# Mirrored inverse rows in both halves of a gated convolution and MLP kernel, with scratch moved and the order lists made anew

## Chip, cores and metric

The kernel runs on one core of one Trainium2 chip. The metric is device time in microseconds (us) for one execution. Times of a kernel are given as the median of its runs; the profile shows one execution.

## The reference, cut

```python
x = A_q                                   # [1, 2048, 640], bf16
g = sigmoid((x * gate_w).sum(-1, keepdims=True))
# A: short causal filter, long causal convolution per channel
k_shift = sum_t k_pad[:, t:t+S, :] * shift_k[:, ks-1-t]      # 4 taps
kv = k_shift * v
y  = irfft(rfft(pad(kv)) * rfft(pad(ssm_k)))[:S] + kv * ssm_D
a  = q * y
# B: layernorm, gelu MLP with shifted column groups, then a second MLP
h  = gelu(layernorm(x) @ w1)              # 640 -> 640
x1 = x + shift_groups(h) @ w2             # groups moved by +1, -1, +2, -2 rows
b  = x1 + gelu(layernorm(x1) @ w3) @ w4   # 640 -> 1536 -> 640
out = g * a + (1 - g) * b
```

## The kernel before

The whole work lies in one SBUF tensor ("arena") with fixed regions. Rows are numbered by r = row mod 8, so each of the 16 row tiles (c = 0, 1 and r = 0 to 7) holds 128 rows.

Branch B is a chain of matrix products: mm1 (layernorm(x) @ w1), mm2 (@ w2), a second layernorm, mm3 (@ w3, line 1064) and mm4 (@ w4, line 1035). The four parts of mm3 and mm4 (sc = 0 to 3) are cut into jobs on TensorE, evicted by ScalarE (line 582).

Branch A does the long convolution by a hand-made transform. The channels are cut into two halves of 320 columns, and each half goes through two parts (kap 0 and 1). Stage numbers in the tags are 2 * half + kap, so stages 0 and 1 are half 0 and stages 2 and 3 are half 1. The steps for a half are:

- forward: TensorE multiplies the taps (h) and kv (k) with a table (line 1093), ScalarE evicts into slots
- window and butterfly (tags win, bhd, bha, bht, bhs for h; bkd, bka, bkt, bks for k): sums and differences of rows on VectorE (line 551)
- product (tags pwT and pwS): the two complex products, with a scratch area "temp" and a result area. An addition inside may be an accumulating DMA on POOL's queue (line 1123; pwTa, pwTb, pwSa, pwSb). The last two instructions of a product (tags ending in z and y) read the scratch
- fold (foldd, folda, foldt, folds): more sums and differences. Where it is done whole, some instructions go through a helper that joins two areas (line 1209)
- inverse (line 1279): for each r0 = 0 to 7, TensorE multiplies rows of the two parts with a table. ScalarE evicts with the gate (gy) into one of four buffers, VectorE multiplies by q (fin) and adds to branch B (finx, or an accumulating DMA fina; finl for the last rows, after mm4 of part 3). An output DMA follows.

A slot has 16 rows of 320 columns. Slots s0 to s4, t0 and t1 lie flat. Slots k0 and k1 are the two column halves of kv's region, so each row of 320 values (640 bytes) is followed by a gap of the same length. The letters a and b name the first and last 8 rows of a slot. q's columns of half 0 are loaded into k0, and of half 1 into k1, by two loads each on SP's queue (line 594); the load for the b rows stands first.

The inverse of a half in EVEN is mirrored: two VectorE passes of 2560 elements (tags mir and mira) form the difference and the sum of the two parts' even rows, and the four even r0 then take two matmul terms of two matmuls each instead of four terms:

```python
mirrored = half in EVEN
if mirrored:
    tt(hs(temp), Y0[0], Y1[0], ALU.subtract, 2560, tag="mir")
    add(Y0[0], Y1[0], 2560, ("mir", half) in BY_DMA, "mira")
```

The fold of part 1 writes its rows in swapped pairs where its half is in EVEN. Scratch for half 1's work depends on half 0:

```python
spare = ("k0a", "k1a", "s1a") if 0 in EVEN else ("s4a", "s4a", "s4a")
units(1, (..., ("pw", 0, spare[0], "s0a", "s4b", "t1a"),
          ..., ("pw", 1, spare[1], "s4b", "t0a", "s3a"), ("fold", 1, "s3b", spare[2])))
inverse(0, Y[0][0], Y[0][1], "s4a")
inverse(1, Y[1][0], Y[1][1], "s3b")
```

The order of all instructions is written out by hand: every operation is a node with its number in order of creation, RANK gives each node its place (highest first), each engine runs its own nodes in that order, and PAIR gives each matmul job one of four pairs of PSUM banks. Semaphore waits follow from which bytes each node reads and writes. Fill matmuls (line 647) stand ahead of the first real work on TensorE.

Of the kernel before, what the change touches and what calls it, by code (L numbers as in the profile page):

```python
# [292 lines left out]
def _bf16_bits(a):  # L293
# [4 lines left out]

FILL = 0
FILLN = 1  # L300
# [14 lines left out]
EVEN = ()  # L315
# [4 lines left out]
EVEN = ()  # L320
# [3 lines left out]
EVEN = (1,)  # L324
# [2 lines left out]
BY_DMA = BY_DMA | {("pwb", 1, 0), ("pwb", 1, 1)}  # L327
R4M = {("h",1),("k",1)}
FILL = 96
PW_SPLIT = ((1, 1),)  # L330
FOLD_SPLIT = ((1, 1),)
LN2_ACT = (2, 3)
RANK = [
# [45 lines left out]
]  # L379
PAIR = [  # L380
# [7 lines left out]
]  # L388

def _freq(kap):  # L390
# [38 lines left out]
def bass_gated_mix__ssm_conv_h3__mixer_s_mlp__prompt_kernel(  # L429
# [98 lines left out]
    def bank(pair, b, n, o=0):  # L528
        c = (2 * pair + b) * 512
        return PS[:, c + o:c + o + n]  # L530
# [113 lines left out]

    for i in range(FILL):
        P.stage = i * 8 // FILL
        P.pe([(lambda e, ps: e.matmul(bank(ps, 0, 128), ones, ones, start=True, stop=True)) for _ in range(FILLN)], r=[ones],
# [674 lines left out]
    def bydma(what, half, kap):  # L1322
        return (what, half, kap) in BY_DMA
# [4 lines left out]
    def units(half, plan):  # L1328
        for step in plan:
# [7 lines left out]
            elif what == "pw":  # L1337
                parts["y"] = [product(parts["bh"][i], parts["bk"][i], step[2 + 2 * i], step[3 + 2 * i],
                                      bydma("pwa", half, kap), bydma("pwb", half, kap), (half, kap) not in PW_SPLIT, "pw" + "TS"[i]) for i in range(2)]
            else:  # L1340
# [55 lines left out]
```

## Time and profile before

| | us |
|---|---|
| median of 3 runs | 227.44 (226.01 to 230.68) |
| the profiled execution | 224.98 |
| its span in the profile | 222.8 |
| TensorE (PE) busy | 214.7 |
| VectorE (DVE) busy | 205.7 |
| ScalarE (ACT) busy | 169.2 |
| GpSimd (POOL) busy | 54.7 |

The span runs from the first to the last instruction of the profiled execution; its time lies 2.2 us above its span. Busy times of one engine's instructions are added without their overlaps. In the groups by line, a helper's line stands for all operations that go through it: 551 for VectorE's two-input operations, 582 for ScalarE's evictions, 1123 for accumulating DMAs, 594 for loads. Lines 1035 (mm4), 1064 (mm3), 1093 (forward) and 1279 (inverse) are the matmuls by job.

### The profile page before, as it was taken

To read this page: it belongs to the slowest core of one execution; us is meant where nothing else is said; L and a number is where in the kernel's file an instruction comes from. 1 tells how busy PE (TensorE), PEld (TensorE's weight loads), DVE (VectorE), ACT (ScalarE), POOL (GpSimd) and SP (SyncE) were. 2 spreads that over 40 slices of the span, in tenths; PEclk is the share of its full clock that TensorE was granted. 3 is DMA by queue.
4 is the path that set the end of the run, shared out by engine and by line. 5 is a ranking of instruction groups with operands and counts; after the bars stand their busy time and mean duration, and the time that the engine had idled before them with its cause. 6 is when DMAs were issued, how large, how long until landed. Compare 5 with 4: busy or idle time off the path is not lost.

```text
span 222.8 us, 3922 instructions
## 1 busy us (share of the span) xinstructions
PE 214.7 (96%) x1533; PEld 135.4 (61%) x1533; DVE 205.7 (92%) x285; ACT 169.2 (76%) x287; POOL 54.7 (25%) x64
## 2 busy tenths in 40 slices
PE   7999999999998899999999999999999999999993
PEld 7749675457666564446765555577554676565671
DVE  2999999999998999999999999999985999998973
ACT  4598997799999999989988998880268342586660
POOL 1143094143015011704200110232310340317200
PEclk9999999999999999999999999999999999999998
DMA  6999985849983778674160154489686489956968
GB/s 205 384 406 389 399 327 105 207 113 259 140 232 108 219 193 299 149 214 90 29 122 0 32 89 87 66 130 188 120 183 174 89 146 175 257 102 107 128 213 261
DMA packets 41578, 39.75 MB, mean 178 GB/s; under 512 B 20452, under 2 KB 34791, under 8 KB 41432
## 3 DMA queue, kind: packets, MB, share of 16 engines
q1 hardware_dynamic: 33864, 24.75, 39.2%
q0 software_dynamic: 7408, 14.42, 31.2%
q10 hardware_dynamic: 288, 0.33, 0.4%
q8 instruction: 12, 0.20, 0.4%
q14 instruction: 6, 0.05, 0.1%
HBM read 21.60 MB, written 3.93 MB: 115 GB/s over the span
## 4 chain that ended last, share of the span: by engine, by line
DVE 49%; PE 32%; DMA 9%; issue 5%; ACT 3%; DVEq 0%; ACTq 0%
DVE arena L551 40%; PE PS L1064 13%; PE PS L1035 9%; PE PS L1093 7%; DMA arena<-arena 7%; DVE arena L778 5%; ACT arena L582 3%; DVE arena L556 2%; PE PS L973 2%; DMA arena<-in_A_q_dram 2%; PE PS L1279 1%; DVE arena L780 1%; DVE arena L1209 1%; ACT PS L955 0%; DVE arena L1048 0%
## 5 line engine op out<-in xcount | busy, mean ns | idle before, releaser
L551 DVE TENSOR_TENSOR arena<-arena 128x1280 bf16<-128x1280 bf16 (+6 forms) x178 | 170.4, 1010 | 7.3 <-DMA arena<-arena 4.9
L582 ACT ACTIVATE arena<-PS 128x640 bf16<-128x640 f32 (+7 forms) x140 | 101.8, 796 | 14.3 <-PE PS L1064 7.3
L1064 PE MATMUL PS<-arena 128*128 128x512 bf16 x240 | 54.3, 379 | 0.2
L1035 PE MATMUL PS<-arena 128*128 128x320 bf16 x384 | 54.3, 299 | 0.1
L582 ACT ACTIVATE arena<-PS,arena 128x320 bf16<-128x320 f32 (+1 forms) x48 | 26.1, 589 | 28.7 <-PE PS L1035 11.8
L1035 PEld LDWEIGHTS PS<-arena 128*128 128x128 bf16 x384 | 37.5, 98 | 15.1 <-issue 0.4
L1123 POOL DMA_DIRECT2D arena<-arena x24 | 24.0, 1172 | 81.3 <-DVE arena L551 75.2
L1064 PEld LDWEIGHTS PS<-arena 128*128 128x128 bf16 x240 | 22.9, 98 | 27.4 <-ACT arena L582 1.2
L1093 PE MATMUL PS<-arena 128*128 128x320 bf16 x208 | 32.3, 299 | 0.4 <-DVE arena L551 0.3
L1093 PEld LDWEIGHTS PS<-arena 128*128 128x128 bf16 x208 | 19.7, 98 | 10.8 <-ACT arena L582 1.1
L568 ACT ACTIVATE arena<-arena 128x640 bf16<-128x640 bf16 (+2 forms) x30 | 22.7, 758 | 2.6 <-DMA arena<-in_A_q_dram 2.2
L973 PE MATMUL PS<-arena 128*128 128x320 bf16 x160 | 22.7, 299 | 1.3 <-ACT PS L955 1.3
L863 PE MATMUL PS<-arena 128*128 128x512 bf16 (+1 forms) x125 | 23.6, 337 | 0.0
L955 ACT ACTIVATE PS<-arena 128x640 f32<-128x640 bf16 x32 | 22.7, 713 | 0.4
L758 POOL TENSOR_TENSOR arena<-arena 128x4 f32<-128x4 f32 (+1 forms) x9 | 13.8, 1531 | 37.0 <-DVE arena L556 34.0
L973 PEld LDWEIGHTS PS<-arena 128*128 128x128 bf16 x160 | 15.2, 98 | 8.6 <-ACT PS L955 2.3
L1279 PE MATMUL PS<-arena 128*128 128x320 bf16 x112 | 17.2, 299 | 0.6 <-DVE arena L551 0.3
L863 PEld LDWEIGHTS PS<-arena 128*128 128x128 bf16 x125 | 11.7, 98 | 9.3 <-ACT arena L582 0.7
L778 DVE BATCH_NORM_STATS2 arena<-arena 128x6 f32<-128x320 bf16 x28 | 12.1, 473 | 3.5 <-DMA arena<-in_A_q_dram 3.5
L1279 PEld LDWEIGHTS PS<-arena 128*128 128x128 bf16 x112 | 10.6, 98 | 6.6 <-ACT arena L582 1.1
L556 DVE TENSOR_SCALAR arena<-arena 128x640 bf16<-128x640 bf16 (+3 forms) x36 | 12.5, 366 | 1.2 <-POOL arena L758 1.0
L903 POOL DMA_DIRECT2D arena<-arena x18 | 9.8, 550 | 10.7 <-ACT arena L582 10.7
(40 smaller groups left out, 77.0 us busy)
## 6 DMA issues: line engine op xcount, KB each, us to landing
arena<-arena POOLq DMA_DIRECT2D x18, 320.0 KB, 4.5
arena<-in_B_w_dram POOLq DMA_DIRECT2D x4, 960.0 KB, 6.4
arena<-in_A_k_dram SPq DMA_DIRECT2D x4, 640.0 KB, 13.1
arena<-in_A_v_dram SPq DMA_DIRECT2D x4, 640.0 KB, 14.1
arena<-arena POOLq DMA_DIRECT2D x4, 640.0 KB, 6.5
arena<-in_A_q_dram SPq DMA_DIRECT2D x4, 640.0 KB, 7.3
out_dram<-arena SPq DMA_DIRECT2D x15, 160.0 KB, 2.0
arena<-in_A_q_dram SPq DMA_DIRECT2D x6, 320.0 KB, 5.1
```

What stands on the lines that cost most here:

```text
L551: return dve(lambda e: e.tensor_tensor(o, a, b, op), [a, b], [o], c_tt(n), tag=tag, **kw)
L568: node = P.op("act", lambda e, ps: e.activation(o, i, func, **kw), r=r, w=[o], cost=c_act(n, naps, acc is not None, psum=False), tag=tag, ...
L582: node = P.op("act", lambda e, ps: e.activation(ov, inner(ps), func, **kw), r=r, w=[o], cost=c_act(n, len(r), acc is not None), job=job, t ...
L778: dve(lambda e, o=o, x=x: e.bn_stats(o, x), [x], [o], 0.393, tag="bn", group=("bn", id(mv), rho, c))
L863: fns.append(lambda e, ps, b=b, c=c, lhsT=lhsT: e.matmul(bank(ps, b, 256 * n), lhsT, XT[:, c, r0:r0 + n, :], start=(c == 0), stop=(c == 4)))
L955: P.seed(job, lambda e, ps: e.activation(two(ps, 320), x, ACTF.Copy), [X[:, c, rho, :]], c_act(640, psum=False), tag)
L973: fns.append(lambda e, ps, hh=hh, ft=ft, lhsT=lhsT: e.matmul(bank(ps, hh, 320), lhsT, w2v[:, ft, 320 * hh:320 * hh + 320], start=False, st ...
L1035: fns.append(lambda e, ps, hh=hh, ft=ft, lhsT=lhsT: e.matmul(bank(ps, hh, 320), lhsT, w4h[ft // 6][:, ft % 6, 320 * hh:320 * hh + 320], st ...
L1064: fns.append(lambda e, ps, b=b, ft=ft, c=c, sc=sc: e.matmul(bank(ps, b, 512), w3h[ft // 6][:, c, 128 * (ft % 6):128 * (ft % 6) + 128], XT[ ...
L1093: fns.append(lambda e, ps, w=w, b=b, rhs=rhs, st=(first and n == 0), en=(n == len(ss) - 1): e.matmul(bank(ps, b, 320), w, rhs, start=st, s ...
L1123: return P.dma("pool", lambda e, ps: e.dma_start(o, i, accum_op=ALU.add, max_dma_last_dim=2560), r=[o, i], w=[o], nbytes=nb, cost=1.2, kin ...
L1279: fns.append(lambda e, ps, w=w, z=z, c=c, st=(n == 0), en=(n == len(terms) - 1): e.matmul(bank(ps, c, 320), w, z[:, c, :], start=st, stop=en))
```

## The change

Half 0 is mirrored like half 1. With it the scratch of half 1's first complex product goes from s4a to k0a (stage 2) and k1a (stage 3), a result area of half 1's second fold goes from s4a to s1a, and s4a holds half 0's difference rows. Half 0's second fold writes its rows in swapped pairs. Two nodes are added (955 become 957), the 244 jobs stay, and both lists are new. Cut diff:

```diff
 FILL = 96
+EVEN = (0, 1)
 PW_SPLIT = ((1, 1),)
 FOLD_SPLIT = ((1, 1),)
 LN2_ACT = (2, 3)
 RANK = [
-    951, 950, 940, 954, 946, 953, 929, 934, 923, 892, 910, 866, 848, 948, 916, 939, 790, 872, 781, 898, 825,
...
+    954, 953, 942, 956, 949, 941, 931, 921, 926, 892, 886, 861, 814, 950, 900, 948, 776, 875, 807, 906, 802,
...
 ]
 PAIR = [
-    0, 1, 2, 2, 2, 1, 0, 3, 3, 2, 2, 2, 1, 0, 1, 1, 2, 2, 3, 1, 2, 3, 0, 0, 3, 2, 3, 3, 1, 1, 2, 0, 1, 0, 3, 3,
...
+    0, 0, 3, 2, 0, 0, 3, 1, 3, 1, 3, 1, 3, 0, 0, 3, 3, 3, 2, 0, 3, 2, 3, 0, 2, 3, 3, 2, 3, 2, 0, 3, 0, 2, 0, 1,
...
 ]
```

VectorE's order from the second half's first butterfly on, before and after, by tag and stage (x counts what stands in a row):

```
before: bhd:2 win:2 folds:1 bht:2x2 win:2 bkd:2 bkt:2 bhd:3 bkt:2 pwT:2 bhs:2 pwT:2x2 bhs:2 pwT:2 bks:2x2 bht:3
  pwS:2x4 bht:3 win:3 pwTy:2 win:3 bht:3 pwTz:2 pwSy:2 bht:3 bhs:3 pwSz:2 bkd:3 foldd:2 bkt:3x4 pwT:3 bhs:3 foldd:2
  bhs:3 pwT:3x4 bks:3x3 fin:0 bhs:3 pwT:3 bks:3 fin:0 pwS:3x5 pwTy:3 pwS:3 pwTz:3 foldt:2 foldd:3 folds:2 pwSz:3
  pwSy:3 foldd:3 foldt:3x2 fin:0x2 folds:3x2 mir:1 mira:1 fin:1x4 finx:1 finl:3x2 ...
after: bhd:2 win:2 bht:2 folds:1 win:2 bht:2 bkd:2 bkt:2 mir:0 mira:0 bhd:3 bkt:2 bhs:2 pwT:2 win:3 bhs:2 pwT:2x3
  bks:2x2 bht:3 pwS:2 bht:3 pwS:2x3 bhs:3 bht:3 bhs:3 pwTy:2 pwTz:2 bht:3 win:3 pwSy:2 pwSz:2 bkd:3 bkt:3x2 foldd:2
  bkt:3x2 foldd:2 pwT:3x4 fin:0 bks:3x2 bhs:3 bks:3 bhs:3 bks:3 pwT:3 pwS:3x5 fin:0 pwT:3 pwTy:3 pwTz:3 foldt:2 pwS:3
  foldd:3 pwSz:3 pwSy:3 foldd:3 folds:2 foldt:3x2 fin:0x2 finl:3 folds:3 fin:1x2 folds:3 mir:1 finl:3 mira:1 ...
```

100 rows, old and new, of tables (PAIR, RANK) are left out of this document.

## Prediction

> **What bounds the kernel now.** I read the page first, then the busy time cut into four stretches, then the waits of VectorE and the chain of waits, and at last the stretch after 139 us instruction by instruction.
>
> ```profile
> span 222.8 us, 3922 instructions
> PE 214.7 (96%) x1533; PEld 135.4 (61%) x1533; DVE 205.7 (92%) x285; ACT 169.2 (76%) x287; POOL 54.7 (25%) x64
> 0.00:71.00 71.00, 68.62 (x615) 47.09 (x615) 66.00 (x101) 61.62 (x109) 21.29 (x33) 1.00 0.84 257
> 71.00:139.70 68.70, 67.31 (x410) 39.03 (x411) 66.70 (x86) 64.18 (x110) 12.96 (x12) 1.00 0.50 124
> 139.70:209.70 70.00, 69.68 (x446) 43.16 (x445) 65.12 (x80) 38.04 (x59) 20.47 (x20) 1.00 0.79 146
> 209.70:222.80 13.10, 9.05 (x66) 6.08 (x63) 7.93 (x20) 5.33 (x11) 0.00 (x0) 0.95 0.72 213
> ```
>
> The columns of the stretches are length, then busy us of PE, weight loads, DVE, ACT and POOL, then clock, DMA share and GB/s. There are two full lanes. TensorE lacks 0.32 us between 139.7 and 209.7 and 1.39 us in the stretch before; VectorE lacks 4.88 us and 2.00 us. Shortening one lane alone buys little, so the change has to be priced on both. Where VectorE idles:
>
> ```profile
> DVE arena L551 <- DMA arena<-arena: 4.9, 4, 3.2
> DVE arena L778 <- DMA arena<-in_A_q_dram: 3.5, 1, 3.5
> DVE arena L556 <- POOL arena L758: 1.0, 1, 1.0
> DVE arena L551 <- PE PS L1093: 0.2, 1, 0.2
> ```
>
> The 4.9 us are waits for accumulating DMAs, and the chain of waits of the last 60 us shows three of them (start, length):
>
> ```profile
> 160.69 1.50 DVE arena L551
> 162.19 0.28 issue
> 162.48 6.87 DMA arena<-arena
> ...
> 191.91 5.67 DMA arena<-arena
> ...
> 200.39 3.60 DMA arena<-arena
> ...
> 205.80 1.50 DVE arena L551
> 207.32 0.71 DVE arena L551
> ...
> 210.71 0.72 PE PS L1279 x4
> 211.43 1.63 PE PS L1035 x12
> ...
> 215.78 3.27 PE PS L1035 x24
> 219.07 0.55 DVE arena L1048
> ```
>
> The instructions at 205.80 and 207.32 are the two mirror passes of half 1 (mir, mira). After them TensorE works through mirrored inverse jobs and half jobs of mm4 until 219.05; a last VectorE instruction and an output DMA end the span at 222.8.
>
> **The change, TensorE lane.** Half 0's four even rows get two terms of two matmuls each where they had four terms: 16 matmuls of 320 columns go. Their price is read from spacing, not from the mean duration, as they overlap:
>
> ```profile
> 143.80 2.34 PE L1279 MATMUL PS<-arena 128*128 128x320 bf16 x16
> 145.97 13.20 PE L1035 MATMUL PS<-arena 128*128 128x320 bf16 x96
> 159.01 6.64 PE L1064 MATMUL PS<-arena 128*128 128x512 bf16 x30
> ```
>
> Sixteen inverse matmuls take 145.97 - 143.80 = 2.17 us, and 96 of mm4 take 13.04 us: 0.136 us each either way. So this lane loses **2.2 us**. In a lane that is idle 0.32 us in 70 this is worth up to all of it. The Trainium skill, page "Perfetto Trace Analysis", section "Identifying the Most-Contended Engine", warns that the busy share of matmuls is a bad measure of distance to the roofline and asks for the weight loads' share; by it the 61% would mean headroom, and the 2.2 us would be worth nothing. The even 0.136 us over 96 matmuls at a clock of 1.00 speaks against headroom here.
>
> **VectorE lane, what is added.** Two passes over 2560 elements in half 0.
>
> ```profile
> L551 DVE TENSOR_TENSOR arena<-arena 128x2560 bf16<-128x2560 bf16 x46 | 68.0, 1487 | 0.8 <-PE PS L1093 0.2
> L1209 DVE TENSOR_TENSOR arena<-arena 128x2560 bf16<-128x2560 bf16 x8 | 11.9, 1486 | 0.1
> ```
>
> Half 1's own pair stands 207.32 - 205.80 = 1.52 us apart, since the second must wait for the first; a pass that nothing waits for costs 1.41 (1.49 less the 0.08 by which neighbours overlap). In the new list the two stand side by side after the second half's bkt, about 8 us behind its first butterfly (bhd of stage 2), where VectorE is full, so they hide under nothing: **+2.9 us**. One fold of half 0 now writes its four rows in reversed pairs through the helper at L1209. No reversed form of that helper is in the trace; its eight instructions cost the same 1.49 us as the plain 2560 ones, and I take no extra. The bound is half rate, +1.4 us, and below nothing is excluded, for the elements are the same.
>
> **VectorE lane, what the new order and the moved scratch do.** The instructions ahead of bhd of stage 2 are the same 186 in both lists. Instructions standing directly behind the one they depend on (0.11 us each: 1.52 less 1.41) fall from 32 to 27, as counted in the two lists: -0.5. The 1.0 us wait for POOL is of the normalisation pass (xn) right behind its square root; in the new list the second kv tail and half 0's butterfly stand between them, so it should go: -1.0. The 0.2 us wait on TensorE's last forward job should go too, because two mm3 jobs (20 matmuls of 512 columns, 20/30 of the 6.47 us from 159.01 to the next job at 165.48, or 4.3 us) are moved behind that job. Half of the 1.7 us could come back as waits that I can't see; I take **-1.1**, from 0 to -1.8.
>
> Next the wait at 169.4:
>
> ```profile
> 162.21 25.54 SPq L594 DMA_DIRECT2D arena<-in_A_q_dram  x4
> 165.48 1.25 PE L1279 MATMUL PS<-arena 128*128 128x320 bf16 x8
> 169.44 1.96 DVE L551 TENSOR_TENSOR arena<-arena 128x1280 bf16<-128x1280 bf16 x3 [3.17 <-DMA arena<-arena]
> 133.38 3.03 DVE L551 TENSOR_TENSOR arena<-arena 128x1280 bf16<-128x1280 bf16 x4 [0.48 <-DMA arena<-arena]
> DMA to landing us min/median/max: 3.6/5.3/7.4
> arena<-in_A_q_dram SPq DMA_DIRECT2D x4, 640.0 KB, 7.3
> arena<-arena POOLq DMA_DIRECT2D x18, 320.0 KB, 4.5
> 197.67 5.49 DVE L551 TENSOR_TENSOR arena<-arena 128x1280 bf16<-128x1280 bf16 x7 [0.31 <-DMA arena<-arena]
> 204.08 6.75 DVE L551 TENSOR_TENSOR arena<-arena 128x1280 bf16<-128x1280 bf16 x9 [0.92 <-DMA arena<-arena]
> ```
>
> VectorE finishes a product at 162.19, POOL issues its accumulate (pwSb) at 162.48, and it lands 6.87 us later, although the least of these accumulates is 3.6. At 162.21 SP was released too, and issued both loads of q's first half, 640 KB each, into k0. They cross it. After the change pwT's scratch lies in k0a. SP's queue keeps its order (k0b's load, then k0a's), but the k0a load must now wait for pwT's last two instructions, which end 3 us later. So one load of two still crosses: 3.60 + half of 3.27 = 5.2 us, between 3.6 and 6.9. Behind the waiting load on SP stand only the loads of q's second half and the outputs. The work between that product and the wait is, in the new list, five instructions of 1280 and two of 640: 5 x 0.74 (four in 3.03 above) + 2 x 0.40 = 4.5 us, against 162.19 to 166.27 before. The wait becomes 0.28 + 5.2 - 4.5 = 1.0 us, from 0 to 2.7: **-2.2**, from -0.5 to -3.2. By the Trainium skill, "DMA: Bandwidth & Descriptors", section "Queues, rings and completion order", each engine alternates between queues packet by packet; the accumulate would then hardly be held, and the wait would be 0. The 6.87 us beside two loads show more holding than that.
>
> Half 1's other two waits on this chain are 0.31 and 0.92 us. The k1a load moves behind pwT of stage 3 in the same way, and so from ahead of pwSa and pwSb there to after them, beside folda. I take -0.6, from +1 (it then crosses folda, whose 3.60 us were undisturbed) to -1.2.
>
> The scratch itself: pwTa of stages 2 and 3 now accumulates into rows of 640 bytes with gaps. The strided and the flat accumulates of before, in the same view:
>
> ```profile
> 144.00:147.00 3.00, 3.00 (x24) 2.17 (x23) 2.97 (x4) 2.50 (x4) 0.00 (x0) 1.00 1.32 180
> 149.00:152.00 3.00, 3.00 (x24) 2.16 (x23) 2.97 (x4) 1.23 (x2) 1.19 (x1) 1.00 1.06 192
> 139.68 2.23 DVE L551 TENSOR_TENSOR arena<-arena 128x2560 bf16<-128x2560 bf16 x2 [0.22 <-PE PS L1093]
> ```
>
> 180 against 192 GB/s is 0.1 us on 320 KB, with some 9 us of products between issue and use: nothing, and 0.1 us if that cover were gone. VectorE's own reads and writes of such rows cost no more: the butterfly on k0, at 139.68, is one of the 46 at 1487 ns.
>
> **Sum.** VectorE: +2.9 - 1.1 - 2.2 - 0.6 = -1.0 at the end of the mirror passes of half 1, with some 1.5 us of later work (two fin, two finl) already drawn ahead of them. TensorE: -2.2, and behind the first mirror pass only four half jobs of mm4 instead of five (1.63 each), besides the same four mirrored jobs. So the tail follows TensorE, less some 0.5 us for gaps between ACT's evictions: **-1.7 us**. The profiled execution would be 223.3 (224.98 before, its span plus 2.2); the median of the three runs, 227.44, is 2.5 above that execution, and I carry the difference over: **225.7 us**.
>
> **Rivals.** (1) VectorE sets the end and its waits return. The passes' 2.9 us stand in full, the lists' saving ahead of bhd fails, and the crossing load still costs 3.17 us: mir ends 2.9 us later, TensorE idles there, and the run is 230.3. It decides once the waits of VectorE on DMAs come to 4.9 us again or more; if k1a's load also holds folda by 3.3 us as q's did pwSb, it is 233.6. For it: VectorE idles only 4.9 us in 70. Against: the two moved scratch areas pull the loads away from two accumulates. The reading of the Trainium skill's page on trace analysis, that TensorE has headroom, would lead here. (2) All waits go: VectorE +2.9 - 1.8 - 4.4 = -3.3, TensorE -2.2 and its 1.4 us of gaps before 139.7: -3.5, or 223.9, and 221.5 with the spread of runs. For it: the lists place mm3 behind the forward jobs, which lets TensorE run ahead. Against: one load of two still crosses. (3) The change does nothing to the end: the matmuls removed are replaced by idling before half 1's inverse, 227.4. For it: the last inverse jobs need half 1's folds, whose date VectorE sets.
>
> **Chances.** Forecast 0.45, rival 1 0.25, rival 2 0.18, rival 3 0.12. 2% is 4.5 us, about what a measurement of this kernel can tell from no change, as its three runs spread over 2%. Faster by over 2% (below 222.9) is two thirds of rival 2 and a little of the forecast: 0.16. Slower by over 2% (above 232) is half of rival 1: 0.13. Within: 0.71. The range goes from rival 2 to the lower case of rival 1: 222.0 to 230.8.
>
> **What would show it.** Right: 96 matmuls at L1279 instead of 112; 48 instead of 46 passes of 2560 at L551; PE's busy time down 2 us, DVE's up 3; the wait before pwSy of stage 2 near 1 us; q's loads spread instead of paired; the last job of mm4 ending near 217.3. Wrong: DVE waits on DMAs at 5 us or more, TensorE idle before half 1's mirrored rows, or new waits of VectorE in the first 140 us, where I assume only that sums stay.

## The result, and the profile after

The changed kernel takes **223.64 us** (median of 4 runs, 223.59 to 224.2) against 226.76 us for the kernel before (4 runs, 226.01 to 230.68): a ratio of 0.9878, 95% interval [0.983, 0.9926]. A second set, with 6 runs against 23, gives 0.9934 [0.9909, 0.9958]. So the change is worth some 0.7% to 1.2%, 1.5 to 3 us, inside 2%. Ratios and intervals leave out runs over 1.5% above the fastest of the same kernel, such as the one of 230.68. Its profiled execution took 224.2 us, 0.8 less than that of before.

The page of the changed kernel and its four stretches (length, then busy us of PE, weight loads, DVE, ACT and POOL, then clock, DMA share, GB/s):

```profile
span 222.3 us, 3888 instructions
PE 213.2 (96%) x1517; PEld 132.8 (60%) x1517; DVE 208.0 (94%) x287; ACT 168.0 (76%) x287; POOL 57.5 (26%) x64
0.00:71.00 71.00, 68.03 (x574) 45.45 (x574) 65.43 (x98) 60.88 (x106) 22.57 (x33) 0.98 0.84 253
71.00:139.70 68.70, 66.67 (x439) 38.45 (x440) 68.46 (x91) 62.83 (x111) 13.66 (x11) 1.00 0.54 130
139.70:209.70 70.00, 69.96 (x445) 43.18 (x444) 65.94 (x82) 38.53 (x59) 21.30 (x20) 1.00 0.82 148
209.70:222.30 12.60, 8.50 (x63) 5.70 (x60) 8.16 (x19) 5.77 (x13) 0.00 (x0) 1.00 0.62 198
```

TensorE is busy 1.5 us less and VectorE 2.3 us more. Two things moved that the sums hide: VectorE does 1.76 us more than before between 71 and 139.7 us (68.46 for 66.70), where it had 2.00 us of room, and TensorE does 0.64 us less there (66.67 for 67.31) but has only 0.04 us of idle time left in the next stretch. The chain of waits shows what that means:

```profile
133.44 1.31 PE PS L1094 x8
134.75 2.21 PE PS L1065 x10
136.96 0.54 PE PS L1094 x4
137.51 10.79 PE PS L1065 x50
148.30 6.52 PE PS L1036 x48
...
201.46 2.35 PE PS L1280 x16
...
215.82 0.56 PE PS L1280 x4
```

(Lines are one higher than before from 330 on: 1280 is the inverse, 1036 mm4, 1065 mm3, 1094 forward, 552 VectorE's two-input operations.) Before, the chain ran through VectorE and three accumulating DMAs from 139.68 to 209.7, and through TensorE only behind that. Now it is TensorE alone from 133.44 to 216.38: behind the last forward job, which starts at 136.96, the chain has no wait but the 0.04 us of an issue. The VectorE passes and the waits that I priced don't lie on it in this execution.

They are close behind it, though. In the profiled execution of the same kernel's second set (its times stand first in the next section), the chain runs through VectorE and the accumulate pwSb until 201.34, and TensorE waits for VectorE there once:

```profile
164.52 6.57 DMA arena<-arena
...
201.39 2.35 PE PS L1280 x16
```

```profile
PE PS L1280 <- DVE arena L552: 0.2, 1, 0.2
```

So in the kernel after the two lanes meet at 201.4 us within 0.2 us of each other, and TensorE alone has the rest.

### The profile page after: what moved, and what is told of

It reads as the page before. It is cut to its first block, busy times and chain, and to the rows that moved or that the text cites. A ratio compares the mean times of both kernels' runs of the same rounds, so it can differ in the third digit from the quotient of the medians.

```text
span 222.3 us, 3888 instructions
## 1 busy us (share of the span) xinstructions
PE 213.2 (96%) x1517; PEld 132.8 (60%) x1517; DVE 208.0 (94%) x287; ACT 168.0 (76%) x287; POOL 57.5 (26%) x64
## 4 chain that ended last, share of the span: by engine, by line
PE 49%; DVE 24%; ACT 17%; DMA 4%; issue 3%; SPq 2%; DVEq 0%; ACTq 0%
PE PS L1036 23%; DVE arena L552 19%; PE PS L1065 17%; ACT arena L583 12%; PE PS L1280 6%; DMA arena<-in_A_q_dram 4%; ACT arena L569 4%; PE PS L1094 3%; DVE arena L779 2%; DVE arena L557 2%; SPq L595 2%; ACT PS L956 1%; DVE arena L781 0%; DVEq L1367 0%; ACTq L1367 0%
## 5 line engine op out<-in xcount | busy, mean ns | idle before, releaser
L552 DVE TENSOR_TENSOR arena<-arena 128x1280 bf16<-128x1280 bf16 (+6 forms) x180 | 173.0, 1014 | 5.6 <-DMA arena<-arena 2.5
L583 ACT ACTIVATE arena<-PS 128x640 bf16<-128x640 f32 (+6 forms) x140 | 103.3, 804 | 19.3 <-PE PS L1065 11.5
L1036 PEld LDWEIGHTS PS<-arena 128*128 128x128 bf16 x384 | 37.5, 98 | 14.8
L1124 POOL DMA_DIRECT2D arena<-arena x24 | 24.9, 1173 | 78.9 <-DVE arena L552 75.9
L1065 PEld LDWEIGHTS PS<-arena 128*128 128x128 bf16 x240 | 23.0, 98 | 27.2 <-ACT arena L583 1.0
L1094 PEld LDWEIGHTS PS<-arena 128*128 128x128 bf16 x208 | 19.1, 98 | 15.2 <-ACT arena L583 4.4
L569 ACT ACTIVATE arena<-arena 128x640 bf16<-128x640 bf16 (+2 forms) x30 | 23.5, 782 | 3.8 <-DMA arena<-in_A_q_dram 2.3
L864 PE MATMUL PS<-arena 128*128 128x512 bf16 (+1 forms) x125 | 24.1, 342 | 0.3 <-DMA arena<-in_B_w_dram 0.3
L974 PEld LDWEIGHTS PS<-arena 128*128 128x128 bf16 x160 | 15.1, 98 | 7.9 <-ACT PS L956 1.4
L864 PEld LDWEIGHTS PS<-arena 128*128 128x128 bf16 x125 | 11.8, 100 | 9.7 <-DMA arena<-in_B_w_dram 1.2
L779 DVE BATCH_NORM_STATS2 arena<-arena 128x6 f32<-128x320 bf16 x28 | 12.7, 475 | 4.2 <-DMA arena<-in_A_q_dram 4.2
L904 POOL DMA_DIRECT2D arena<-arena x18 | 9.8, 549 | 11.2 <-ACT arena L583 11.2
L1210 DVE TENSOR_TENSOR arena<-arena 128x2560 bf16<-128x2560 bf16 x8 | 11.9, 1484 | 0.1
```

What stands on the lines that cost most here:

```text
L552: return dve(lambda e: e.tensor_tensor(o, a, b, op), [a, b], [o], c_tt(n), tag=tag, **kw)
L569: node = P.op("act", lambda e, ps: e.activation(o, i, func, **kw), r=r, w=[o], cost=c_act(n, naps, acc is not None, psum=False), tag=tag, ...
L583: node = P.op("act", lambda e, ps: e.activation(ov, inner(ps), func, **kw), r=r, w=[o], cost=c_act(n, len(r), acc is not None), job=job, t ...
L779: dve(lambda e, o=o, x=x: e.bn_stats(o, x), [x], [o], 0.393, tag="bn", group=("bn", id(mv), rho, c))
L864: fns.append(lambda e, ps, b=b, c=c, lhsT=lhsT: e.matmul(bank(ps, b, 256 * n), lhsT, XT[:, c, r0:r0 + n, :], start=(c == 0), stop=(c == 4)))
L974: fns.append(lambda e, ps, hh=hh, ft=ft, lhsT=lhsT: e.matmul(bank(ps, hh, 320), lhsT, w2v[:, ft, 320 * hh:320 * hh + 320], start=False, st ...
```

## What each part is worth in the new list

The four runs of this section change one part of the kernel after.

**The kernel after once more.** 

> The changed kernel once more, beside the others on one chip: 223.6 us by its four runs, 0.988 of the kernel before. All theories expect the same.

Measured: 224.27 us, ratio 0.9934 [0.9909, 0.9958].

**The new list without mirrored rows in half 0.**

```diff
-EVEN = (0, 1)
+EVEN = (1,)
-    P.schedule(RANK, PAIR)
+    P.schedule([x for i, x in enumerate(RANK) if i not in (840, 841)], PAIR)
```

> The new order alone: half 0 isn't mirrored (112 inverse matmuls, no passes for it), its scratch is as before, and the order is the new one with the two passes taken out. Theory: TensorE is the lane that sets the end, so the 16 matmuls (2.2 us) come back and the passes' 2.9 us on VectorE buy nothing: 225.0 to 226.5 us, 1.4 to 2.2 above the changed kernel (223.6). Rival A, VectorE sets the end: 2.9 us below the changed kernel, 220.7. Rival B, the new order made the whole gain: 223.6, as the changed kernel.

Measured: 225.81 us, ratio 1.0001 [0.9973, 1.0029], in the theory's range and in neither rival's. The list alone gains nothing, and against the kernel after, measured in the same set, it lacks 1.5 us (1.0001 less 0.9934). Its chain of waits is TensorE's too, with the last forward job 0.4 us earlier than in the kernel after and 2 us more work behind it:

```profile
136.56 0.54 PE PS L1094 x4
...
217.38 0.56 PE PS L1280 x4
```

**Two terms of half 0's even rows multiplied twice.**

```diff
-                terms = [(GM[:, 0, ri, r, s, :], src[ri]) for ri in range(2)]
+                terms = [(GM[:, 0, ri, r, s, :], src[ri]) for ri in range(2)] * (2 - half)
```

> The changed kernel with the 16 matmuls back: each of the two terms of half 0's even rows is multiplied twice, so those rows come out doubled; passes, scratch and order stay. Theory: TensorE sets the end, 16 x 0.136 = 2.2 us above the changed kernel: 225.8 to 226.5. Rival, VectorE sets the end: no more than 0.5 us above it.

Measured: 225.41 us, ratio 0.9988 [0.9958, 1.0017], a little below the theory's range and above the rival's. With the 16 matmuls back the gain is gone: 1.2 us by the two ratios (0.9988 less 0.9934). Its chain:

```profile
136.72 0.54 PE PS L1094 x4
...
217.54 0.56 PE PS L1280 x4
```

From the last forward job to the last inverse job it is 80.82 us, as in the list without mirrored rows (217.38 - 136.56 = 80.82), and 78.86 in the kernel after (215.82 - 136.96): the 16 matmuls make a difference of 1.96 us on TensorE's lane, of which 1.2 to 1.5 show in the ratios.

**Half 0 without its two passes.**

```diff
-        if mirrored:
+        if half == 1:
```

The places of the two passes leave the list, as in the run without mirrored rows.

> The changed kernel without half 0's two mirror passes: half 0's even rows are computed from the unmirrored parts and stale scratch, the 96 inverse matmuls stay. VectorE does 2.9 us less. Theory: TensorE sets the end from 134 us on, VectorE has room there, so 0 to 0.6 us below the changed kernel (223.6 to 224.3 in its two sets of runs). Rival, VectorE sets the end: 2.9 us below it, 221.

Measured: 224.0 us, ratio 0.9926 [0.9898, 0.9953], the ratio of the kernel after within the intervals. In the new list two passes of 1.5 us on an engine that is busy 94% cost nothing that the times can tell. The trace has a little:

```profile
137.98 0.54 PE PS L1094 x4
...
216.63 0.56 PE PS L1280 x4
```

That is 78.65 us from the last forward job to the last inverse job, 0.21 less than in the kernel after. So VectorE holds TensorE up by 0.2 us there and no more, and without that wait the 16 matmuls are worth 80.82 - 78.65 = 2.17 us of the lane, the prediction's 2.2.

## The same parts in the old list

**Mirrored rows and moved scratch in the list of before.** The two passes stand behind the last fold of stage 1 (folds), and three operations that would come ahead of one that they depend on are moved behind it.

```diff
-EVEN = (1,)
+EVEN = (0, 1)
+    rank = list(RANK)
+    rank[840:840] = [rank[687] - 0.3, rank[687] - 0.6]
-    P.schedule(RANK, PAIR)
+    P.schedule(repaired(rank), PAIR)
```

> Both halves mirrored with the scratch moved, in the old order (the two passes stand behind the last fold of half 0; three places are mended where the moved scratch forces an instruction back). Theory: TensorE loses 2.2 us of matmuls but its first inverse job stands right behind the fold and must wait for the passes, about 2.5 us: 226.0 to 227.5. Rival A, VectorE sets the end: the passes' 2.9 us less 1 to 2 us of shorter waits: 227.7 to 228.7. Rival B, order makes the whole gain: as before, 226.8.

Measured: 228.4 us, ratio 1.0131 [1.01, 1.0162], slower than the theory's 226.0 to 227.5 and in the range of rival A, VectorE. The same edit to the computation that gains 0.7% in the new list loses 1.3% in the old one. Its chain is VectorE's with the accumulates, as before:

```profile
165.51 0.28 issue
165.80 6.41 DMA arena<-arena
...
202.83 3.61 DMA arena<-arena
...
208.25 1.50 DVE arena L551
```

The pass that stood at 205.80 (mir of half 1) stands at 208.25, 2.45 us later, and TensorE waits for VectorE (PE behind DVE, line 1279) in the view of waits:

```profile
PE PS L1279 <- DVE arena L551: 3.1, 3, 1.4
PE PS L1279 <- ACT arena L582: 1.1, 2, 0.8
```

Two more runs ask whether VectorE's chain is the whole cause.

**The same without half 0's passes.** 

> As mirror_old_order (both halves mirrored, scratch moved, the list of before), but without half 0's two mirror passes: its even rows are made from what lies in the scratch. Theory (in the old list VectorE's chain sets the end, so the two passes are paid in full there, while the new list hides them under TensorE): ratio 0.990 to 0.997, that is 3.5 to 5 us below mirror_old_order, the chain of waits ending as that of the moved scratch alone. Rival (the old list does not fit the mirrored rows for another reason, TensorE's shorter jobs of half 0 waiting for ACT's evictions or for VectorE's products): at least 1.003, with TensorE still idle 3 us or more after 139.7.

Measured: 225.51 us, ratio 0.9992 [0.9969, 1.0014]: 1.4% less than with the passes, 3.1 us for two passes that I had at 2.9. In the old list they are paid in full. The theory's number was missed on the high side, though: what remains has no gain that shows, although 16 matmuls are gone. Its chain is still VectorE's, and TensorE's lane has 1.2 us of idle time ahead of half 1's rows, so a part of the 2.2 us removed is spent waiting (the profiled execution took 226.34 us, more than the median, and its last forward job came 1.1 us later than that of before, so its dates are late as a whole):

```profile
163.67 6.43 DMA arena<-arena
...
206.16 1.50 DVE arena L551
```

```profile
PE PS L1279 <- DVE arena L551: 1.2, 1, 1.2
```

**The same with the passes, and q's first loads behind pwSy of stage 2.** 

> As mirror_old_order with its two passes, and both loads of q's first half behind pwSy of stage 2. Theory (VectorE's chain sets the end in the old list): the wait of 2.7 us before pwSy goes and the end with it, ratio 1.001 to 1.006 instead of 1.0131. Rival (TensorE's idle time before half 0's rows, 2.0 us at 143.7 and 145.5, is what reaches the end): 1.010 to 1.014.

Measured: 225.9 us, ratio 1.0001 [0.9979, 1.0024]. The other way to take 3 us out of VectorE's chain gives back the same 1.3%, a shade more than the theory's range. The rival is out as the cause of that 1.3%: TensorE's wait before half 0's rows is still there, and the end moved all the same.

```profile
PE PS L1279 <- DVE arena L551: 1.8, 2, 1.0
```

It counts for what remains, however. The chain of this run goes through half 0's two passes, which end at 147.67, and from there on through TensorE. With 16 matmuls more, no passes in half 0, the scratch of before and the same edit of the loads, the old list stands at 0.9942 (the same edit in the kernel before, below). So by these runs the mirrored rows lose on both lanes in the old list: on VectorE's chain, and once that is relieved by TensorE's wait for the passes.

## The load that crosses the accumulate

**Only the scratch moved, in the list of before.**

```diff
-    spare = ("k0a", "k1a", "s1a") if 0 in EVEN else ("s4a", "s4a", "s4a")
+    spare = ("k0a", "k1a", "s1a")
```

> Only the scratch of half 1's products and one result area of its fold are moved (k0a, k1a, s1a); half 0 isn't mirrored, the order is the old one but for the instructions that the moved scratch forces back. Theory: TensorE sets the end and its work is the same, so the time is that of before within 0.7 us, while VectorE's wait before pwSy of stage 2 falls from 3.2 us to 1 to 2.5 us. Rival A, VectorE sets the end: faster by what the wait falls, 1 to 2 us. If the loads were not what held that accumulate, the wait stays at 3.2.

Measured: 224.93 us, ratio 0.9961 [0.994, 0.9982], so 0.9 us, just outside the theory's 0.7 and just short of rival A's 1 to 2. The loads of q's first half are now issued apart, at 162.60 and 166.68, and the accumulate pwSb of stage 2 in the chain of waits still takes 6.34 us (6.87 before); the wait behind it is 2.65 us instead of 3.17, and not in the 1 to 2.5 that I expected:

```profile
162.87 6.34 DMA arena<-arena
```

**The kernel after, with both loads of q's first half behind pwSy of stage 2.**

```diff
+    rank = list(RANK)
+    for i, n in enumerate((839, 838)):       # the two loads
+        P.nodes[n].deps.add(P.nodes[781])    # pwSy of stage 2
+        rank[n] = rank[781] - 0.3 - 0.3 * i
-    P.schedule(RANK, PAIR)
+    P.schedule(rank, PAIR)
```

> The changed kernel with both loads of q's first half held until the accumulate that they cross has been used (they wait for pwSy of stage 2). The wait of VectorE ahead of that instruction should fall from 2.2 us to 0.3 or less, if the crossing load is what holds the accumulate; if it is not, the wait stays. Theory, TensorE sets the end: the time stays within 0.5 us of the changed kernel, and VectorE waits later instead. Rival, VectorE sets the end: 2 us faster, 222.

The accumulate pwSb alone, in the view of its line's instructions between 163.5 and 165.3 us (the first row of the kernel after, the second of this run):

```profile
DMA to landing us min/median/max: 6.3/6.3/6.3
```

```profile
DMA to landing us min/median/max: 3.6/3.6/3.6
```

Measured: 223.77 us, ratio 0.9923 [0.9897, 0.9948]. The accumulate lands after 3.6 us, VectorE's wait ahead of pwSy is gone, and the time stays that of the kernel after. VectorE waits later instead, for ACT:

```profile
DVE arena L552 <- ACT arena L583: 3.7, 3, 2.8
```

What holds the accumulate can be read from the packets by DMA queue (packets, MB, share of the 16 engines; q0 is POOL's queue, q1 the loads'). First the kernel after, where the loads are issued at 164.54 and 167.55 and the accumulate at 164.81. The rows are those of 165.5 to 168.2 us and of 169 to 170 us:

```profile
q1 hardware_dynamic: 550, 0.35, 58.2%
q0 software_dynamic: 22, 0.02, 4.1%
...
q0 software_dynamic: 67, 0.17, 89.6%
q1 hardware_dynamic: 70, 0.04, 19.7%
```

Then the run with both loads behind pwSy, 166 to 167.5 us, its accumulate issued at 164.4:

```profile
q0 software_dynamic: 113, 0.29, 104.9%
```

Once it moves, the accumulate has most of the DMA engines with or without a load beside it (89.6% and 104.9%): the two queues send about as many packets, 67 and 70, and the accumulate's are larger. What it loses is mostly its start. Alone its data flow from 1.6 us behind the issue; behind the load they begin at about 168.2, 3.4 us behind it, when the load has moved 0.35 MB. That is 1.8 us of the 2.7 that it lands later; the other 0.9 go while both move. In the kernel before it is the same, 0.38 MB of the loads alone in the window from 163.5 to 165.9:

```profile
q1 hardware_dynamic: 594, 0.38, 65.5%
```

**The same edit in the kernel before.** 

> The kernel before with one edit: both loads of q's first half wait for the second product sum (pwSy) of stage 2, so that neither crosses the accumulate before it. Theory (the crossing loads cost the kernel before about 1 us at the end: VectorE waits there, TensorE then waits before half 1's inverse rows; scratch moved alone gained 0.9 to 1.1): wait before pwSy falls from 3.17 us to at most 0.3, accumulate 3.6 us instead of 6.9, TensorE's gap of 0.7 us before half 1's inverse goes, ratio 0.992 to 0.997. Rival (the gain of the moved scratch was not the load's crossing, but where tiles lie or noise): wait gone, accumulate 3.6, time within 0.3% of before.

Measured: 224.33 us, ratio 0.9942 [0.9919, 0.9966]. That is in the theory's range: one dependency of two loads brings the kernel before to a ratio inside the interval of the second set of the whole change. The chain of waits tells why:

```profile
139.31 0.54 PE PS L1093 x4
139.86 4.32 PE PS L1064 x20
...
215.06 3.27 PE PS L1035 x24
```

From the last forward job on it has left VectorE for TensorE. So in the kernel before VectorE's chain set the end, and TensorE's lane lay 1.3 us (0.58% of 225.6) behind it.

## The date of TensorE's last forward job

**What the new list does ahead of bhd of stage 2 in the order of before, the rest as after.** The edit is the two lists alone.

> The changed kernel with the old order for everything that the new order puts ahead of the first butterfly of the second half, and the new order behind it; one matmul job gets another PSUM pair. TensorE then works off its first 138 us as before, but with the two mm3 jobs (4.3 us) behind, where the new order has them. Theory, TensorE sets the end and loses 2.1 us of those 4.3 to new gaps in the new head: 1 to 2 us faster than the changed kernel, 222 to 223. Rival, VectorE sets the end: its wait of 1.0 us on POOL and the 0.5 us of dependent pairs come back, 0.5 to 1.5 us slower, 224.5 to 225.5.

Measured: 226.03 us, ratio 1.0019 [0.9997, 1.004]. Neither number was right: it is 2 us slower than the kernel after. TensorE's last forward matmuls start at 136.8 in both kernels, so the job comes no earlier than there: TensorE waits 1.8 us for evictions up to it, and behind it 1.2 us more. Its second stretch and its waits (lines are ten higher here: 1103 forward, 1074 mm3, 592 ScalarE's evictions):

```profile
71.00:139.70 68.70, 64.67 (x393) 36.87 (x392) 67.42 (x86) 63.09 (x107) 12.31 (x12) 1.00 0.52 126
```

```profile
PE PS L1103 <- ACT arena L592: 1.8, 3, 1.2
PE PS L1074 <- ACT arena L592: 1.2, 2, 0.8
```

TensorE is busy 2.0 us less there than in the kernel after. The two mm3 jobs that the new list draws behind the last forward job had been filling the time in which TensorE waits for evictions. Taken from between the forward jobs of the old order they leave a hole; in the new order of these jobs they don't. That is read from the trace; no run moved those two jobs alone.

**The kernel with q's loads moved, and the gate jobs drawn into TensorE's gap at 69 us.** Besides the edit of the loads:

```diff
+    for k, i in enumerate((345, 346, 343, 344)):   # the two gate jobs
+        RK[i] = RK[594] + 0.8 - 0.2 * k            # ahead of k's first forward job
```

One matmul job takes another PSUM pair by it.

> The changed kernel with q's first loads behind pwSy of stage 2, as in q_behind, and the two gate jobs (20 one-column matmuls each) drawn ahead of the first forward job of k, where TensorE waits 1.2 to 1.7 us for VectorE at about 69 us. Theory (the end is the date of TensorE's last forward job plus its work behind that, so filling a TensorE gap ahead of that job moves the end): 0.5 to 1.2 us less than q_behind, ratio to before 0.984 to 0.990. Rival (the gap is set by VectorE's date, and what follows it on TensorE waits for VectorE again; the matmuls moved were never in the way): as q_behind, 0.990 to 0.995.

Measured: 223.71 us, ratio 0.9916 [0.9888, 0.9945]. In the profiled executions the last forward job starts 0.9 us earlier than with the loads alone (136.55 there) and so does the last inverse job (215.20 there):

```profile
135.66 0.54 PE PS L1094 x4
...
214.31 0.56 PE PS L1280 x4
```

The span is 220.8 us against 221.7. The medians differ by 0.06 us, inside both intervals, and the ratio lies in the rival's range and not in the theory's: the trace has the theory's shift, the times can't tell it from nothing. This is the lowest of the ratios measured beside 22 or more runs of before, but it isn't shown to beat the kernel after.

## Why the prediction came out where it did

The forecast for the profiled execution was 1.7 us less than before, and the ratios have 1.5 (0.9934) to 2.8 (0.9878) us less. The size and the statement that the tail follows TensorE hold. Point by point:

- **TensorE, -2.2 us.** Right. 96 matmuls at the inverse's line, as said (first row):

```profile
L1280 PE MATMUL PS<-arena 128*128 128x320 bf16 x96 | 15.0, 299 | 0.0
L552 DVE TENSOR_TENSOR arena<-arena 128x2560 bf16<-128x2560 bf16 x48 | 71.2, 1495 | 0.6
L1210 DVE TENSOR_TENSOR arena<-arena 128x2560 bf16<-128x2560 bf16 x8 | 11.9, 1484 | 0.1
```

  Shown by putting them back: 2.17 us of the lane where VectorE holds nothing up, 1.2 to 1.5 us in the ratios. The reading of the Trainium skill that I weighed (page "Perfetto Trace Analysis", "Identifying the Most-Contended Engine"), by which weight loads at 60% would mean headroom, does not hold here.
- **The passes, +2.9 us on VectorE.** Right in size (the old list pays 3.1 for them), and two more 2560-element rows as said (second row above). The rows in reversed pairs cost nothing extra, as I took it (third row, 1484 ns against 1486). But my sum added the passes to one lane and took the wait off the same lane; in the new list that lane reaches the end by 0.2 us at most, and leaving the passes out gains nothing that the times can tell.
- **Ahead of bhd of stage 2, -1.1 us.** Measured -1.6: the first row below starts it at 138.08 (139.68 before). The wait for POOL and that for TensorE's last forward job went, as said.

```profile
138.08 2.96 DVE L552 TENSOR_TENSOR arena<-arena 128x2560 bf16<-128x2560 bf16 x3
171.24 3.09 DVE L552 TENSOR_TENSOR arena<-arena 128x1280 bf16<-128x1280 bf16 x3 [2.25 <-DMA arena<-arena]
203.52 0.83 DVE L552 TENSOR_TENSOR arena<-arena 128x1280 bf16<-128x1280 bf16 x1 [0.21 <-DMA arena<-arena]
205.40 3.16 DVE L552 TENSOR_TENSOR arena<-arena 128x640 bf16<-128x640 bf16 x4 [1.05 <-ACT arena L583]
```

- **The wait before pwSy of stage 2, -2.2 us: mis-sized.** It went from 3.17 to 2.25 (second row above), so -0.9. The step that failed is that one crossing load of two holds the accumulate half as long (5.2 us). The hold is for the most part the delay of the accumulate's start by the load issued 0.3 us ahead of it, and that load still goes ahead; moving the other 3 us back leaves 6.3 us of 6.87. The rule of the Trainium skill that I set beside it (page "DMA: Bandwidth & Descriptors", "Queues, rings and completion order") agrees with the trace while both move, 67 packets against 70. What I drew from it, a wait of 0, fails since it says nothing of the start. That this wait decides anything holds only in the old list, where its removal is worth 1.3 us.
- **Half 1's other waits, -0.6.** 0.31 and 0.92 became 0 and 0.21, so -1.0. Right behind them VectorE now waits 1.05 us for an eviction (last row above); that this came late since TensorE was is likely, but no run shows it.
- **What the sum left out: TensorE's own date.** I let two mm3 jobs move behind the last forward job and counted only VectorE's part of it. In the trace the chain of the kernel after has 50 mm3 matmuls in a row behind that job, where the kernel before with its loads moved has 20. The job starts 2.4 us earlier (136.96 against 139.31), and the list alone gives nothing back. By the two runs that bound it, the new list costs TensorE's lane 1.3 us against the old one (order alone 1.0001, old list with TensorE at the end 0.9942). The traces of these two have it as well. The first row below is TensorE's last of the list alone, the second that of the kernel before with its loads moved, the third that of the kernel after:

```profile
217.97 1.79 PE L1036 MATMUL PS<-arena 128*128 128x320 bf16 x12
214.89 3.42 PE L1035 MATMUL PS<-arena 128*128 128x320 bf16 x24
216.41 1.79 PE L1036 MATMUL PS<-arena 128*128 128x320 bf16 x12
```

  With the list alone TensorE ends 83.2 us behind its last forward job (136.56), with the old list 79.0 behind it (139.31): 4.2 us more work, about the 4.3 of the two jobs, for a start 2.75 us earlier. The matmuls return 1.2 to 2.2 us, and VectorE's lane gets the room for the passes. My -1.7 came out of other terms than the ones that made it, so that the size came out near is in part luck; and the last mm4 job, which I had ending near 217.3, ends at 218.2 (third row).
- **From the profiled execution to the median.** I carried 2.5 us over. Later sets of 22 to 28 runs put the median of before at 225.6 to 226.0, 0.6 to 1.0 above its profiled execution; with that the forecast would have been about 224.

The ends of my range, 222.0 and 230.8, are not those of the rivals' sums (223.9 or 221.5, and 230.3); nothing hangs on it here.

Rival 1 (VectorE sets the end, 230.3) is what the old list does with this change, at 228.4. Rival 3 (the matmuls removed turn into idling before half 1's rows) is near to what the old list does without the passes, at 0.9992. Rival 2's 223.9 lies nearer to the first set's median than my 225.7, but for a reason that didn't occur: of the waits it takes away, the one before pwSy still holds 2.25 us. Why the gain in the profiled executions (0.8 us) is smaller than in the medians isn't settled; the profiled execution after had a clock of 0.98 in its first stretch where before had 1.00.

## What to carry to other kernels

When two engines are both over 90% busy, find out which lane sets the end, and how far behind the other lies, by relieving each alone: here one dependency that kept two loads off an accumulate showed that VectorE's chain ended 1.3 us later than TensorE's. An edit that trades one lane's work for the other's is worth the first lane's saving only with an order that leaves room in the second: the same mirrored rows gave +1.3% in the old list and -0.7% in the new one. Price a reordering on the engine that ends last, by the date of its last job with an outside dependency plus the work behind it, and not by sums of waits on the other.

## What the runs showed of the hardware beyond what I expected

A 320 KB accumulating DMA on POOL's queue lands after 3.6 us with no load beside it, 6.3 us behind one 640 KB load issued 0.3 us ahead of it with the next 3.0 us later, and 6.87 us beside two, one issued 0.3 us ahead of it and one 0.4 us behind it. Two thirds of the difference between the first two lie ahead of its first packet (3.4 us behind the issue instead of 1.6), and only the rest in the stretch in which both move. Keeping only the later load away gained 0.6 us, keeping both away gained 3.3. Why the start waits for the load isn't settled.
